# Two rows of a query weight kept on chip, and a new order of PV and scores, in a decode kernel that streams a KV cache

## The chip, the core and the metric

One core of a Trainium2 chip. The metric is the device time of one launch in microseconds. The kernel before takes 1152.5 us (median of 3 runs, 1148.8 to 1153.3).

A *ratio* below is the mean time of one kernel's fast runs over that of the kernel before in the same rounds, so it is not quite the ratio of the medians that are quoted with it. Differences in us are (ratio - 1) x 1152.

## The reference

```python
x = A_x                                        # 8 x 1 x 512
for _ in range(2):                             # two layers, same weights and same caches
    x = x + attn(layernorm(x), A_k_cache, A_v_cache, A_wq, A_wo)
    x = x + ffn(layernorm(x), B_w1, B_w2)      # silu(x @ w1) @ w2, 512 -> 1792 -> 512
# attn: 32 query heads, 8 KV heads, 8192 positions, head size 128, all 8 batches at one token
```

K and V are 134 MB each. The kernel reads K once for both layers, V twice, and runs the first layer of batch b+1 together with the second layer of batch b.

## The kernel before

All engines are filled from a static list. A planner in Python gives each piece of work a modelled duration and a priority, plays the kernel through, and the instructions are emitted in the order that comes out. Loads go out in a fixed order on one queue. V, `wo` and `wq` rows land in a ring of 7 cells of 512 KB (4 KB per partition); two neighbouring free cells may take one load of 1 MB. A cell comes free when the PV matmuls on it are done.

```python
N_CELL = 7
...
def load_wq(half, kt):          # one row of wq: 512 KB, one ring cell
    return load_cells(f"wq{half}.{kt}", 1, [(lambda buf: buf, wq_v[:, kt, GR * half:GR * (half + 1)])])
...
PARK = [(OT[0], ("ot", 0)), (OT[1], ("ot", 1)), (YT, ("yt",)), (EX, ("ex",))]   # spare halves of 4 PSUM banks
...
def queries_1(tag, prio, b0, nb, deps):         # queries of heads 16..31
    for kt in range(KT):                        # 4 rows of wq
        parked = kt == KT - 1 and nb == 1       # nb == 1: second layer of one batch
        wn = plan.reserve(f"{tag}.wq1") if parked else load_wq(1, kt)
        ...                                     # a parked row: 4 DVE transposes from PSUM to the cell
...
# in keys(): scores of one unit (batch, head group), four groups of 8 matmuls
sn.append(plan.add(f"s{u}.{q}", "PE", 0.45, score, pr - 1, [tn[3], bn] + sn[-1:]))
...
# in values(): PV of one unit, four groups of 8 matmuls, one for each cell
pr = count[0] - 1 if b < NB - 1 else u + 1
...
# in the planner: a node's followers become ready HOP = 0.1 us after it, on its own engine too
if what == "free":
    free[n.eng] = True
    heapq.heappush(events, (now + self.HOP, seq, "done", n))
```

## Time and profile before

| | before |
|---|---|
| time, median | 1152.5 us |
| profiled run: span, bytes on the queue | 1152.9 us (time 1154.7), 460.90 MB |
| busy: PE, DVE, ACT | 63%, 53%, 12% |
| queue's share of the 16 DMA engines | 98.1% |
| wq row loads into the ring | 28 |

The kernel streams: read the DMA and GB/s rows first, then ask in which stretches the rate is below the best. The prediction shows the lines.

### The profile page before, as it was taken

To read this page: it belongs to the slowest core of one execution; us is meant where nothing else is said; L and a number is where in the kernel's file an instruction comes from. 1 tells how busy PE (TensorE), PEld (TensorE's weight loads), DVE (VectorE), ACT (ScalarE), POOL (GpSimd) and SP (SyncE) were. 2 spreads that over 40 slices of the span, in tenths; PEclk is the share of its full clock that TensorE was granted. 3 is DMA by queue.
4 is the path that set the end of the run, shared out by engine and by line. 5 is a ranking of instruction groups with operands and counts; after the bars stand their busy time and mean duration, and the time that the engine had idled before them with its cause. 6 is when DMAs were issued, how large, how long until landed. Compare 5 with 4: busy or idle time off the path is not lost.

```text
span 1152.9 us, 32289 instructions
## 1 busy us (share of the span) xinstructions
PE 727.5 (63%) x13900; PEld 389.1 (34%) x13900; DVE 613.5 (53%) x1772; ACT 139.7 (12%) x485; POOL 116.8 (10%) x295
## 2 busy tenths in 40 slices
PE   2544565675665856656665766567566575665886
PEld 1322332342332433324332333234233243332544
DVE  5653467625674366634667255752566436663341
ACT  0010011101111110111111111110111111011111
POOL 1000111101110010100111000110011001010110
PEclk9655667757776676756767576765777566675675
DMA  9999899999999999999999999999999999999993
GB/s 368 419 422 399 326 416 424 413 403 409 423 417 411 396 423 418 417 389 412 417 419 417 397 417 419 419 410 394 417 421 417 403 412 421 415 419 396 369 424 135
DMA packets 78446, 462.96 MB, mean 402 GB/s; under 512 B 8400, under 2 KB 10208, under 8 KB 51936
## 3 DMA queue, kind: packets, MB, share of 16 engines
q1 hardware_dynamic: 78304, 460.90, 98.1%
q8 instruction: 109, 1.79, 0.6%
q14 instruction: 33, 0.27, 0.1%
HBM read 460.86 MB, written 0.01 MB: 400 GB/s over the span
## 4 chain that ended last, share of the span: by engine, by line
DMA 71%; PE 22%; issue 3%; DVE 2%; SPq 1%; POOL 1%; ACT 0%; POOLq 0%; DVEq 0%; ACTq 0%
DMA ring<-in_A_v_cache_dram 68%; PE ot L964 10%; PE sc L838 5%; DMA w<-in_B_w_dram 1%; PE misc L698 1%; PE misc L566 1%; DMA ring<-in_A_wq_dram 1%; PE misc L548 1%; PE yt L1038 1%; PE ex L986 1%; DVE part L978 0%; SPq L386 0%; PE sc L813 0%; POOL rstd L513 0%; PE ex L1008 0%
## 5 line engine op out<-in xcount | busy, mean ns | idle before, releaser
L964 PE MATMUL ot<-ring,p 128*8 128x256 bf16 x3904 | 246.1, 364 | 195.3 <-DMA ring<-in_A_v_cache_dram 191.3
L783 DVE STREAM_TRANSPOSE kts<-kts 128x1024 uint32<-128x1024 uint32 x256 | 308.5, 1225 | 32.1 <-DMA kts<-in_A_k_cache_dram 31.5
L838 PE MATMUL sc<-kts,bd 128*32 128x256 bf16 x4096 | 297.7, 406 | 38.9 <-DVE kts L783 32.8
L964 PEld LDWEIGHTS ot<-ring,p 128*8 128x8 bf16 x3904 | 79.1, 93 | 275.8 <-DMA ring<-in_A_v_cache_dram 247.4
L838 PEld LDWEIGHTS sc<-kts,bd 128*32 128x32 bf16 x4096 | 113.1, 118 | 109.3 <-DVE kts L783 45.7
L978 DVE TENSOR_TENSOR part<-ot,p 128x256 bf16<-128x256 f32 x128 | 54.2, 423 | 170.3 <-PE sc L838 80.4
L855 POOL PARTITION_ALL_REDUCE small<-small x128 | 47.6, 372 | 612.9 <-DVE small L851 382.0
L864 ACT ACTIVATE expd<-sc,small 128x256 bf16<-128x256 f32 x128 | 60.6, 473 | 403.9 <-DVE small L859 298.0
L974 ACT ACTIVATE p<-ot 128x256 bf16<-128x256 f32 x128 | 49.0, 383 | 458.1 <-PE ot L964 457.1
L870 PE MATMUL sc<-expd,ident 128*32 128x256 bf16 x512 | 43.1, 325 | 82.0 <-ACT expd L864 81.8
L884 POOL PARTITION_ALL_REDUCE small<-small x128 | 55.7, 435 | 213.8 <-DVE small L880 213.8
L877 DVE STREAM_TRANSPOSE p<-sc 128x256 bf16<-128x256 bf16 x128 | 56.6, 442 | 17.3 <-PE sc L870 13.8
L850 DVE TENSOR_REDUCE small<-sc 128x1 f32<-128x256 f32 x128 | 53.2, 416 | 18.1 <-PE sc L838 18.1
L821 DVE TENSOR_TENSOR bd<-sc,mask 128x64 bf16<-128x64 f32 x128 | 27.7, 216 | 54.9 <-PE sc L838 50.0
L870 PEld LDWEIGHTS sc<-expd,ident 128*32 128x32 bf16 x512 | 15.3, 110 | 110.7 <-ACT expd L864 109.2
L1015 DVE TENSOR_TENSOR z<-ex,rc 128x16 bf16<-128x16 f32 x72 | 12.5, 174 | 64.9 <-PE ex L1008 64.8
L880 DVE TENSOR_SCALAR small<-hm,small 128x4 f32<-128x4 f32 x128 | 26.6, 208 | 28.8 <-ACT expd L864 28.3
L986 PE MATMUL ex<-diag,p 128*128 128x4 bf16 x256 | 25.7, 169 | 25.4 <-DVE part L978 21.5
L986 PEld LDWEIGHTS ex<-diag,p 128*128 128x128 bf16 x256 | 16.9, 104 | 68.3 <-ACT p L974 41.5
L1038 PEld LDWEIGHTS yt<-z,ring 128*128 128x128 bf16 x1024 | 31.7, 102 | 24.2 <-issue 24.1
L1038 PE MATMUL yt<-z,ring 128*128 128x4 bf16 x1024 | 36.6, 166 | 4.7 <-DVE z L1015 4.3
L859 DVE SCALAR_TENSOR_TENSOR small<-small,hm 128x4 f32<-128x4 f32 x128 | 18.5, 144 | 26.4 <-POOL small L855 25.5
(96 smaller groups left out, 530.2 us busy)
## 6 DMA issues: line engine op xcount, KB each, us to landing
ring<-in_A_v_cache_dram SPq DMA_DIRECT2D x136, 1024.0 KB, 11.4
kts<-in_A_k_cache_dram SPq DMA_DIRECT2D x64, 2048.0 KB, 10.9
ring<-in_A_v_cache_dram SPq DMA_DIRECT2D x216, 512.0 KB, 7.5
ring<-in_A_wo_dram SPq DMA_DIRECT2D x64, 512.0 KB, 11.7
ring<-in_A_wq_dram SPq DMA_DIRECT2D x28, 512.0 KB, 10.4
kts<-in_A_v_cache_dram SPq DMA_DIRECT2D x5, 2048.0 KB, 23.9
kts<-in_A_wo_dram SPq DMA_DIRECT2D x2, 2048.0 KB, 16.4
w<-in_B_w_dram SPq DMA_DIRECT2D x2, 1792.0 KB, 13.7
```

The costliest lines, as they stand in the source:

```text
L783: op(dve, lambda: dve.transpose(v, v), reads=[], writes=[res("kt", g)], add=(q > 0))
L838: steps.append(lambda t=t, y=y, w=w: pe.matmul(sc[32 * t:32 * t + 32, 0:256], w, kv[:, 2 * t + y, q], start=(q == 0 and y == 0), stop=(q = ...
L850: op(dve, lambda: dve.tensor_reduce(mxr[si], sv, AX.X, ALU.max), reads=[res(*scr)], writes=[res("mxr", si)])
L864: op(act, lambda: act.activation(pe_out[:, :], sv, ACT.Exp, bias=bias[si], scale=SM_SCALE, accum_out=rsum[si]), reads=[res(*scr), res("bia ...
L870: steps = [lambda P=P: pe.matmul(sc[32 * P:32 * P + 32, 256:512], src[:, P], pe_out[:, :], start=True, stop=True) for P in range(4)]
L877: op(dve, lambda: dve.transpose(pt[:, :], src), reads=[res(*scr)], writes=[res("p", sm)])
L884: op(pool, lambda: pool.partition_all_reduce(ssa[si], ssm[si], 128, bass.bass_isa.ReduceOp.add), reads=[res("mxp", si)], writes=[res("mxa" ...
L964: steps.append(lambda t=t, c=c, k=k: pe.matmul(ot[32 * t:32 * t + 2 * R, 0:2 * DH], pt[:, k:k + 2 * R], vt[:, c, t], start=(P == 0 and c = ...
L974: op(act, lambda: act.activation(pt[:, :], ot[:, 0:2 * DH], ACT.Copy), reads=[res("ot", o)], writes=[res("p", sm)])
L978: op(dve, lambda: dve.tensor_tensor(part[:, :], ot[:, 0:2 * DH], pt[:, :], ALU.subtract), reads=[res("ot", o), res("p", sm)], writes=[res( ...
L986: steps.append(lambda k=k, src=src, y=y: pe.matmul(EX[:, 0:R], src[:, y * DH:y * DH + DH], diag[:, R * y:R * y + R], start=(k == 0 and y = ...
L1038: steps.append(lambda j=j, dt=dt: pe.matmul(YT[:, dt * R:(dt + 1) * R], w[:, j, dt * 128:(dt + 1) * 128], zt[:, R * j:R * j + R], start=(g ...
```

## The change

Its intent: fewer bytes, and cells that come back sooner.

1. Of the four rows of the second half of `wq`, two are kept on chip instead of one: in six pieces in spare columns of PSUM, and in 768 bytes per partition of SBUF. The exponential's own buffer, 512 bytes, was given up for these: the exponential now writes straight to its final buffer `p`. Two rows are loaded per batch, not three, and the four rows are used in a new order (3, 2, 0, 1).
2. They come back by four ACT copies and two DVE copies. Their cells are taken when they are needed (`extra`), not in the load order.
3. PV gets a better priority by three units: PV of landed values goes ahead of scores.
4. A node's followers on its own engine are ready at once, so the four score groups of a unit run through; their modelled duration goes from 0.45 to 0.5 us.
5. The first queries of a batch come in three groups instead of two.

```diff
+    def extra(self, name, emit, deps):                  # a cell without a load
...
             if what == "free":
                 free[n.eng] = True
+                for o in n.outs:
+                    if o.eng == n.eng:
+                        o.left -= 1
+                        if o.left == 0:
+                            heapq.heappush(heaps[o.eng], (o.prio, pending[id(o)], o))
...
-        for g0, g1 in ((0, 1), (1, 4)):
+        for g0, g1 in ((0, 1), (1, 2), (2, 4)):
...
+    PARK = [(3, 0, 256, OT[0], ("ot", 0), 256), (3, 256, 256, OT[1], ("ot", 1), 256),
+            (3, 512, 480, YT, ("yt",), 32), (3, 992, 32, EX, ("ex",), 480),
+            (2, 0, 448, EX, ("ex",), 32), (2, 448, 384, MI, ("misc",), 128)]
...
-        for kt in range(KT):
-            parked = kt == KT - 1 and nb == 1
+        rows = (3, 2, 0, 1)
+        for kt in rows:
+            kept_at = [i for i in range(len(PARK)) if PARK[i][0] == kt]
+            if kept_at and nb == 1:
+                wn = take_cell(kt, deps + list(behind))
...
-            sn.append(plan.add(f"s{u}.{q}", "PE", 0.45, score, pr - 1,
+            sn.append(plan.add(f"s{u}.{q}", "PE", 0.5, score, pr - 1,
...
-            op(act, lambda: act.activation(pe_out[:, :], sv, ACT.Exp, ...
+            op(act, lambda: act.activation(pt[:, :], sv, ACT.Exp, ...
...
-        pr = count[0] - 1 if b < NB - 1 else u + 1
+        pr = count[0] - 4 if b < NB - 1 else u + 1
```

More of the change, by code (lines that the diff above doesn't have):

```diff
@@ L118 @@
     __slots__ = ("eng", "dur", "emit", "prio", "deps", "outs", "left", "ready", "end", "take", "give", "name", "cells",
-                 "mate", "span")
+                 "mate", "span", "clear")
     def __init__(self, name, eng, dur, emit, prio, deps):
@@ L153, in __init__ @@
         self.loads = []
+        self.extras = []
     def add(self, name, eng, dur, emit, prio, deps=()):
@@ L167, in load @@
         return n
-    def reserve(self, name):
-        n = self.load(name, 1, lambda: None)
-        n.dur = 0
+    def extra(self, name, emit, deps):
+        n = Node(name, "DMA", 0, emit, 0, deps)
+        n.take = True
+        n.cells = 1
+        self.nodes.append(n)
+        self.extras.append(n)
         return n
@@ L198, in run @@
         loads = list(self.loads)
+        extras = list(self.extras)
         li = 0
@@ L211, in run @@
                 moved = False
+                for n in extras:
+                    at = self.place(idle, 1) if n.left == 0 else None
+                    if at is not None:
+                        extras.remove(n)
+                        n.give = at
+                        idle.discard(at)
+                        order.append((now, seq, n))
+                        seq += 1
+                        heapq.heappush(events, (now + self.HOP, seq, "done", n))
+                        seq += 1
+                        moved = True
+                        break
                 if li < len(loads):
@@ L242, in run @@
                         seq += 1
-                        if dur:
-                            wire = max(wire, now + 0.1) + dur
-                        heapq.heappush(events, (wire + self.LAND if dur else now + self.HOP, seq, "done", n))
+                        wire = max(wire, now + 0.1) + dur
+                        heapq.heappush(events, (wire + self.LAND, seq, "done", n))
                         seq += 1
@@ L277, in run @@
                 for o in n.outs:
+                    if o.eng == n.eng and n.eng != "DMA":
+                        continue
                     o.left -= 1
@@ L305, in _build @@
     NCH = 64
+    W1 = 384
     pe, dve, act, pool, sp = nc.tensor, nc.vector, nc.scalar, nc.gpsimd, nc.sync
@@ L337, in _build @@
     bds = [sb([128, 4 * 48], BF16, f"bd{i}") for i in range(N_BD)]
-    pe_out = sb([128, NCH * R], BF16, "expd")
+    wq1 = sb([128, W1], BF16, "wq1")
     ps = [sb([128, NCH * R], BF16, f"p{i}") for i in range(N_P + N_DEF)]
@@ L466, in norm_nodes @@
     def norm_nodes(tag, prio, b0, nb, deps):
-        nm = MI[:, 472:472 + nb]
-        st = MI[:, 480:480 + nb]
-        sq = MI[:, 488:488 + nb]
+        at = 40 if nb == 1 else 472
+        nm, st, sq = (MI[:, at + 8 * k:at + 8 * k + nb] for k in range(3))
         bs = slice(b0, b0 + nb)
@@ L539, in ffn_nodes @@
         hp = MI[:, 0:FT * nb]
-        yp = MI[:, 256:256 + KT * nb]
+        yp = MI[:, 32:32 + KT] if nb == 1 else MI[:, 256:256 + KT * nb]
         th, hs = (th1[:, :], hs1[:, :]) if nb == 1 else (big_th[:, 0:FT * nb], big_hs[:, 0:FT * nb])
@@ L709, in queries_0 @@
         return out_n
-    PARK = [(OT[0], ("ot", 0)), (OT[1], ("ot", 1)), (YT, ("yt",)), (EX, ("ex",))]
+    PARK = [(3, 0, 256, OT[0], ("ot", 0), 256), (3, 256, 256, OT[1], ("ot", 1), 256),
+            (3, 512, 480, YT, ("yt",), 32), (3, 992, 32, EX, ("ex",), 480),
+            (2, 0, 448, EX, ("ex",), 32), (2, 448, 384, MI, ("misc",), 128)]
     parks = []
-    def parked(i):
-        return PARK[i][0][:, 256:512].bitcast(U32)
-    def piece(wn, i):
-        n = GR // len(PARK)
-        return gran(wn.give)[:, n * i:n * (i + 1)].bitcast(U32)
@@ L722, in park @@
-    def park(i, wn):
-        op(dve, lambda: dve.transpose(parked(i), piece(wn, i)), reads=cells_of(wn), writes=[res(*PARK[i][1])])
-    def unpark(i, wn):
-        op(dve, lambda: dve.transpose(piece(wn, i), parked(i)), reads=[res(*PARK[i][1])],
-           writes=cells_of(wn), add=i > 0)
-    def queries_1(tag, prio, b0, nb, deps):
+    def park(i, wn):
+        row, w0, n, bank_, key, c0 = PARK[i]
+        op(dve, lambda: dve.tensor_scalar(
+            bank_[:, c0:c0 + n].bitcast(U32), gran(wn.give).bitcast(U32)[:, w0:w0 + n], 0, None, op0=ALU.bitwise_or),
+            reads=cells_of(wn), writes=[res(*key)])
+        if key == ("misc",):
+            op(dve, lambda: dve.tensor_copy(wq1[:, :], gran(wn.give)[:, GR - W1:GR]), reads=cells_of(wn), writes=[res("wq1")])
@@ new lines, in unpark @@
+    def unpark(i, wn, eng):
+        row, w0, n, bank_, key, c0 = PARK[i]
+        syn.acquire(eng, [wn.clear], [res(*key)])
+        if eng is act:
+            inst = act.activation(
+                gran(wn.give)[:, 2 * w0:2 * (w0 + n)], bank_[:, c0:c0 + n].bitcast(BF16), ACT.Copy)
+        else:
+            inst = dve.tensor_scalar(
+                gran(wn.give).bitcast(U32)[:, w0:w0 + n], bank_[:, c0:c0 + n].bitcast(U32), 0, None, op0=ALU.bitwise_or)
+        tok = syn.mark(inst, eng)
+        syn.release(tok, (), [res(*key)])
+        syn.release(tok, (), cells_of(wn), add=True)
@@ L732, in queries_1, with take_cell, emit @@
+    def take_cell(row, deps):
+        n = plan.extra(f"wq1.{row}", None, deps)
+        def emit():
+            n.clear = Res("clear")
+            for c in cells_of(n):
+                n.clear.writes += c.writes + c.reads
+                c.writes, c.reads = [], []
+        n.emit = emit
+        return n
+    def queries_1(tag, prio, b0, nb, deps, behind=()):
         qp = MI[:, 0:16 * nb]
         last = []
-        for kt in range(KT):
-            parked = kt == KT - 1 and nb == 1
-            wn = plan.reserve(f"{tag}.wq1") if parked else load_wq(1, kt)
-            filled = [wn]
-            if parked:
-                for i in range(len(PARK)):
-                    filled.append(plan.add(
-                        f"{tag}.unpark{i}", "DVE", 0.4, lambda i=i, wn=wn: unpark(i, wn), prio,
-                        [parks[i], filled[-1]]))
+        rows = (3, 2, 0, 1)
[3 more added lines that the diff above has]
+                wn = take_cell(kt, deps + list(behind))
+                eng, name = (act, "ACT") if kt == 3 else (dve, "DVE")
+                filled = [wn]
+                for i in kept_at:
+                    filled.append(plan.add(
+                        f"{tag}.unpark{i}", name, (0.3 + PARK[i][2] / 600) if eng is act else (0.1 + PARK[i][2] / 950),
+                        lambda i=i, wn=wn, eng=eng: unpark(i, wn, eng), prio, [wn, parks[i]] + filled[1:]))
+            else:
+                wn = load_wq(1, kt)
+                filled = [wn]
@@ L746, in mul @@
                 for h in range(16):
-                    steps.append(lambda h=h: pe.matmul(
-                        qp[:, h * nb:(h + 1) * nb], gran(wn.give)[:, h * DH:(h + 1) * DH], xn[:, b0:b0 + nb, kt],
-                        start=(kt == 0 and h == 0), stop=(kt == KT - 1), skip_group_check=True))
-                mms(steps, reads=cells_of(wn) + [res("xn")], writes=[res("misc")], add=kt > 0)
-            last = [plan.add(f"{tag}.r{kt}", "PE", 0.5, mul, prio, filled + deps + last)]
-            if kt == KT - 1 and nb > 1:
-                for i in range(len(PARK)):
-                    parks.append(plan.add(
-                        f"{tag}.park{i}", "DVE", 0.4, lambda i=i, wn=wn: park(i, wn), prio + 8,
-                        [wn, clear_n, last[0]] + parks[-1:]))
-                frees(parks[-1], wn)
+                    w = gran(wn.give)[:, h * DH:(h + 1) * DH]
+                    if kt == 2 and nb == 1 and (h + 1) * DH > GR - W1:
+                        w = wq1[:, h * DH - (GR - W1):(h + 1) * DH - (GR - W1)]
+                    steps.append(lambda h=h, w=w: pe.matmul(
+                        qp[:, h * nb:(h + 1) * nb], w, xn[:, b0:b0 + nb, kt],
+                        start=(kt == rows[0] and h == 0), stop=(kt == rows[-1]), skip_group_check=True))
+                mms(steps, reads=cells_of(wn) + [res("xn"), res("wq1")], writes=[res("misc")], add=kt != rows[0])
+            last = [plan.add(f"{tag}.r{kt}", "PE", 0.5, mul, prio, filled + deps + last)]
+            if kept_at and nb > 1:
+                done = last[0]
+                for i in kept_at:
+                    done = plan.add(f"{tag}.park{i}", "DVE", 0.1 + PARK[i][2] / 950, lambda i=i, wn=wn: park(i, wn),
+                                    prio + 8, [wn, clear_n, done])
+                    parks_of[i] = done
+                frees(done, wn)
             else:
                 frees(last[0], wn)
+        if nb > 1:
+            parks[:] = [parks_of[i] for i in range(len(PARK))]
         n = plan.add(f"{tag}.qc4", "DVE", 0.17, lambda: query_copy(4, 8, qp, nb), prio, last)
         return {g: n for g in range(4, 8)}
+    parks_of = {}
     count = [0]
     plain = [0]
-    last_exp = []
     sc_users = []
@@ L863, in exp @@
         def exp():
-            op(act, lambda: act.activation(pe_out[:, :], sv, ACT.Exp, bias=bias[si], scale=SM_SCALE, accum_out=rsum[si]),
-               reads=[res(*scr), res("bias", si)], writes=[res("expd"), res("rsum", si)])
+            op(act, lambda: act.activation(pt[:, :], sv, ACT.Exp, bias=bias[si], scale=SM_SCALE, accum_out=rsum[si]),
+               reads=[res(*scr), res("bias", si)], writes=[res("p", sm), res("rsum", si)])
         def swap():
@@ L870, in swap @@
             steps = [lambda P=P: pe.matmul(
-                sc[32 * P:32 * P + 32, 256:512], src[:, P], pe_out[:, :], start=True, stop=True) for P in range(4)]
-            mms(steps, reads=[res("ident"), res("expd")], writes=[res(*scr)])
+                sc[32 * P:32 * P + 32, 256:512], src[:, P], pt[:, :], start=True, stop=True) for P in range(4)]
+            mms(steps, reads=[res("ident"), res("p", sm)], writes=[res(*scr)])
         def back_in():
@@ L895, in keys @@
         n3 = plan.add(f"own{u}", "DVE", 0.17, own_max, pr - 1, [n2])
-        n4 = plan.add(f"exp{u}", "ACT", 0.42, exp, pr, [n3] + last_exp)
+        n4 = plan.add(f"exp{u}", "ACT", 0.42, exp, pr, [n3] + p_users.get(sm, []))
         n5 = plan.add(f"ss{u}", "DVE", 0.17, ssum, pr - 2, [n4])
         m4 = plan.add(f"sw{u}", "PE", 0.3, swap, pr - 2, [n4])
-        last_exp[:] = [m4]
-        n4 = plan.add(f"bk{u}", "DVE", 0.45, back_in, pr - 2, [m4] + p_users.get(sm, []))
+        n4 = plan.add(f"bk{u}", "DVE", 0.45, back_in, pr - 2, [m4])
         n6 = plan.add(f"sa{u}", "POOL", 0.45, sall, pr, [n5])
@@ L1064, in own @@
                 mask[:, :].unsqueeze(1).to_broadcast([128, R * nb, R]), ALU.mult),
-                reads=[res("ex"), res("mask")], writes=[res("ring", 1)])
+                reads=[res("mask")], writes=[res("ex"), res("ring", 1)])
         def mul():
@@ L1180, in advance @@
                     if g == 4:
-                        second_q.update(queries_1(f"c{b}", count[0] - 3, b, 1, [ready, second_q[3]]))
+                        second_q.update(queries_1(f"c{b}", count[0] - 3, b, 1, [ready, second_q[3]], scored[1]))
                     made[k] = keys(1, kb, g, second_q[g], held_units.index(k) if k in held_units else None, g == 0)
@@ L1203, in _build @@
     w = free_yt[0]
-    done = [h["n"] for h in ends] + [made[1]["n"]]
+    done = [h["n"] for h in ends] + [made[1]["n"], second_q[G - 1]]
     for g in range(G):
```

## The prediction

> **What bounds the kernel now.** I read the front page first: the slices, the DMA queue and the transfers.
>
> ```profile
> DMA  9999899999999999999999999999999999999993
> GB/s 368 419 422 399 326 416 424 413 403 409 423 417 411 396 423 418 417 389 412 417 419 417 397 417 419 419 410 394 417 421 417 403 412 421 415 419 396 369 424 135
> ...
> q1 hardware_dynamic: 78304, 460.90, 98.1%
> ...
> ring<-in_A_v_cache_dram SPq DMA_DIRECT2D x136, 1024.0 KB, 11.4
> ...
> ring<-in_A_v_cache_dram SPq DMA_DIRECT2D x216, 512.0 KB, 7.5
> ring<-in_A_wo_dram SPq DMA_DIRECT2D x64, 512.0 KB, 11.7
> ring<-in_A_wq_dram SPq DMA_DIRECT2D x28, 512.0 KB, 10.4
> ```
>
> The 16 DMA engines are full in all slices but the fifth and the last, and they move 460.90 MB. No compute engine is near that: PE is busy 63% of the span, DVE 53%, ACT 12%. Bytes divided by rate therefore give most of the 1152.9 us. The next view, stretches of 20 us, shows where they do not; its last three columns are the granted PE clock, the DMA share and GB/s.
>
> ```profile
> 100.00:120.00 20.00, 9.46 (x237) 6.85 (x238) 3.19 (x13) 1.32 (x6) 1.15 (x2) 0.50 0.99 373
> 120.00:140.00 20.00, 11.79 (x236) 6.78 (x236) 9.26 (x25) 1.78 (x6) 1.62 (x4) 0.67 0.77 311
> ...
> 420.00:440.00 20.00, 12.46 (x229) 6.89 (x232) 12.77 (x35) 2.45 (x8) 2.03 (x5) 0.69 1.02 419
> ...
> 500.00:520.00 20.00, 12.81 (x245) 6.10 (x241) 4.66 (x19) 2.44 (x9) 1.40 (x3) 0.50 1.01 379
> ...
> 640.00:660.00 20.00, 13.72 (x299) 7.41 (x300) 3.82 (x16) 2.09 (x8) 1.03 (x2) 0.56 1.01 401
> ...
> 1080.00:1100.00 20.00, 17.92 (x344) 9.45 (x348) 9.09 (x46) 3.91 (x14) 3.21 (x8) 0.83 0.98 355
> ...
> 1120.00:1140.00 20.00, 15.78 (x359) 10.04 (x359) 3.62 (x15) 2.48 (x9) 1.53 (x1) 0.50 0.68 283
> 1140.00:1160.00 20.00, 6.17 (x164) 4.92 (x162) 2.53 (x9) 0.94 (x4) 0.55 (x1) 0.63 0.00 1
> ```
>
> Three levels are to be seen. Where K and paired V come in (2 MB and 1 MB), the rate is about 419. Where single cells of 512 KB come in, around the change from one batch to the next, it is about 400 although the share is still 1.01. Real holes are few: about 5 us in 120 to 140 (one minus 0.77, times 20; rate 311), about 2 us in 100 to 120, about 3 us in 1080 to 1100 (one minus 355/419, times 20), and the end. In 1120 to 1140 the rate of 283 gives 5.66 MB, at 420 some 13.5 us, so the last bytes land near 1134. The kernel ends at 1152.9: a tail of about 19 us in which DMA does nothing.
>
> **What holds the queue.** The waits of the DMA queue itself:
>
> ```profile
> SPq L91 <- PE ot L964: 582.0, 285, 19.9
> SPq L386 <- PE sc L838: 121.6, 19, 14.2
> SPq L91 <- PE yt L1038: 43.3, 22, 2.8
> ```
>
> The issuing sequencer spends half the span waiting for PV matmuls to give ring cells back. This looks like the bound, but it is back-pressure: with a share of 1.0 the engines still have earlier transfers to do while the sequencer waits. Only where the share or the rate drops is such a wait worth time.
>
> **What the Trainium skill says.** "DMA: Bandwidth & Descriptors", section "Rules for kernel authors", asks for 128 partitions and at least 1 MiB per DMA for the best bandwidth. The trace agrees in direction: 419 against 401 GB/s, a loss of 4% for 512 KB; so a saved wq row is dearer than its bytes suggest. "Perfetto Trace Analysis", section "Optimization Strategy", says to look for the gaps on the most contended engine; that is what the second view was for. "ScalarE: Activation LUTs", section "What ACT_TABLE_LOAD costs", gives an ACTIVATE with immediate scale and bias as 186 ns + 0.833 N. At N = 256 that is 399 ns; the copy of PV's result (128x256) takes 383 ns here, so I use it for the new ACT copies. "PSUM — Partial Sum Buffer", section "PSUM bank collisions raise a hardware error", says to guard PSUM by bank and quadrant, not by address: copies out of spare columns must be ordered against the matmuls that write other columns of that bank. The code does acquire the bank; no run so far shows what that wait costs.
>
> **The change part by part.**
>
> (a) *Bytes.* Before, one of the four rows of the second half of wq was parked in PSUM and three were loaded for each batch: 4 at the start plus 8 times 3 = 28, as the transfer list has it. After, two are kept. The issue order of the changed kernel has 20. Eight transfers of 524,288 bytes go: 4.19 MB, at 400 GB/s 1.31 us each, 10.5 us together. The order also has V in 133 pairs and 222 singles where it was 136 and 216: six singles more (7.9 us) for three pairs less (3 x 2.50 = 7.5 us), +0.4 us. Net -10.1 us on an engine that is full there, so this comes off the end nearly whole. w1 and w2 are loaded by the same two statements in both kernels; I give that nothing.
>
> (b) *Unparking.* Before: four DVE transposes of 128x256 words for each batch, 32 x about 408 ns = 13 us in all. After: four ACT copies (512, 512, 960 and 64 elements: by the formula 0.61, 0.61, 0.99, 0.24, an estimate of 2.45 us per batch, 20 us in all) and two DVE copies of 448 and 384 words (estimate from the transposes of 256 words at 408 ns: 0.6 us each, 10 us in all). ACT goes from 139.7 to about 160 us busy, DVE falls slightly. The cells for them are taken when they are needed, after the first scores of the batch, instead of in the load order; in the new order this puts the next V pair a few instructions later, right behind a 2 MB K load that covers 5 us. I give 0 to +1 us per batch at worst, 0 as the centre.
>
> (c) *Order on PE.* PV of landed cells now goes before scores, and the four score groups of a unit run together. This gives cells back sooner. It is worth only what starvation there is: in the batch changes (379 in 500 to 520 against 400 possible is 1 us; others less) and in 1080 to 1100 (3 us). I count -2 us. The hole at 120 to 140 stays: there are no held units to fill the first feed-forward, and the new order has the same two V pairs and then the same K load that waits for the first unit's scores.
>
> (d) *The tail.* The timeline of the end before:
>
> ```profile
> 1130.70 1.65 PE L566 MATMUL misc<-ring,w 128*128 128x7 bf16 x56
> ...
> 1132.29 1.45 PE L964 MATMUL ot<-kts,p 128*8 128x256 bf16 x24
> ...
> 1136.49 1.45 PE L964 MATMUL ot<-kts,p 128*8 128x256 bf16 x24
> ...
> 1139.98 0.60 PE L964 MATMUL ot<-kts,p 128*8 128x256 bf16 x8
> ...
> 1143.37 0.17 DVE L1109 TENSOR_REDUCE ysum<-yt 128x4 f32<-128x16 f32 x1 [0.68 <-PE yt L1038]
> ```
>
> The last value quarter is in by about 1134, but its 8 matmuls run at 1139.98: PE is about 6 us behind with PV of the last three units and with the other seven batches' feed-forward put between. In the new order, all 32 PV matmuls of the third last unit stand before that feed-forward's first half, and 64 instead of 96 PV matmuls follow it. If PE keeps up, the last PV follows its landing within 1.5 us and the tail shrinks by about 4.5 us; the chain behind it (3.4 us to the sum, 9.5 us of feed-forward and output) stays. PE is busy 17.9 of 20 us just before, so it may not keep up: I count -2.5.
>
> Sum: 1152.5 - 10.1 + 0 - 2 - 2.5 = about 1138.
>
> **The rivals.** *Only the bytes count* (the tail order is eaten by PE at its low clock, 0.50 in that window; ring cells were never the limit): 1142. For it: share 1.01 almost everywhere. Against it: the 6 us lag at the end is real, and the order view shows a real change there. *Cells become the bound*: two cells held for unparking while ACT does 2.4 us of copies behind its exponentials, PE's scores of later units blocked behind an in-order wq matmul, each batch starving DMA by 2 us: 8 x 2 = 16 us lost, 1154. For it: the 582 us of waits for cells show how tight the ring is. Against it: before, loaded rows held their cells some 10 us each from issue to landing, so two loaded plus two short-lived cells ask for less than three plus one. *The order pays more than I think*: all batch changes rise to 400 to 405, the 3 us near 1085 vanish, the first hole shrinks by half and the tail by 4.5: about 1152.5 - 10.1 - 6 - 3 - 4.5 = 1129, just at 2%.
>
> **Range and chances.** The bytes are nearly certain and make 0.9%. The range runs from most of the third rival to somewhat worse than the first: 1131 to 1147, which also covers the 4.6 us spread of the three runs before. Over 2% faster means below 1129.5, possible only if every side effect pays: 0.08. Over 2% slower would need 23 us of new waiting on top of the lost saving: 0.02.
>
> **What would show it.** Right: 456.7 MB on the queue, 20 wq transfers in the ring, the same level of about 419 and 400 in the same kinds of stretch, last bytes near 1122 to 1124, and the last PV within 2 us of them. (c) wrong: 1080 to 1100 still near 355. (d) wrong: still 18 us or more after the last bytes. The whole is wrong if the DMA share falls below 0.95 in stretches with unparking, or if the queue's waits show a new line for ACT or for the clearing of a wq cell.

## More of the kernel before

One more view is needed for the result, and the prediction did not have it: the stretches in which one batch gives way to the next. I bounded them by K loads, whose 16,384-byte packets can be told apart: from the landing of a batch's last K to that of the next batch's first. Here are four of the six, in the kernel before; the columns are the stretch, its length, busy us and instructions of PE, PE's weight loads, DVE, ACT and POOL, then the granted PE clock, the DMA share and GB/s.

```profile
217.10:269.30 52.20, 34.19 (x684) 18.38 (x684) 17.67 (x62) 6.41 (x22) 4.38 (x10) 0.62 1.01 400
...
491.10:542.80 51.70, 34.63 (x684) 18.25 (x684) 17.58 (x62) 6.33 (x22) 4.37 (x10) 0.57 1.01 397
628.40:678.60 50.20, 34.13 (x684) 18.41 (x684) 17.60 (x62) 6.33 (x22) 4.38 (x10) 0.60 1.02 404
...
901.10:951.80 50.70, 33.69 (x684) 18.65 (x684) 17.56 (x61) 6.33 (x22) 4.38 (x10) 0.60 1.02 408
```

To be seen: the DMA share says "full" in all of them, while the rate differs by 11 GB/s between stretches that move the same kinds of transfer. The share alone does not tell the faster stretch from the slower.

## The result, and the profile after

1148.8 us (median of 4 runs, 1148.0 to 1149.8) against 1151.6 in the same rounds: ratio 0.9978, 95% interval 0.9955 to 1.0001. A second measurement in other rounds gave 0.9964 (0.9945 to 0.9983). So the change is worth 2.5 to 4 us (the first interval just includes none), not the 14 that I predicted, and the time lies above my range.

From the page of the changed kernel, the queue and its transfers:

```profile
q1 hardware_dynamic: 77584, 456.70, 98.0%
...
ring<-in_A_v_cache_dram SPq DMA_DIRECT2D x133, 1024.0 KB, 11.7
...
ring<-in_A_v_cache_dram SPq DMA_DIRECT2D x222, 512.0 KB, 7.3
...
ring<-in_A_wq_dram SPq DMA_DIRECT2D x20, 512.0 KB, 12.2
```

The bytes went as predicted: 4.20 MB less, 20 wq loads, 133 pairs and 222 singles. Stretches of 20 us of the changed kernel, to be set against those in the prediction:

```profile
120.00:140.00 20.00, 12.90 (x273) 7.74 (x270) 10.46 (x29) 3.73 (x10) 1.62 (x4) 0.59 0.76 294
...
640.00:660.00 20.00, 14.93 (x344) 8.77 (x347) 4.03 (x17) 1.92 (x7) 1.15 (x2) 0.50 1.02 401
...
1060.00:1080.00 20.00, 17.22 (x428) 11.93 (x429) 6.34 (x27) 4.05 (x11) 1.38 (x3) 0.59 0.91 343
```

The hole of the first change of batch is as deep as before, and the dip of 1080 to 1100 has moved to 1060 to 1080 and is no smaller: 343 against 355. (A second profile of the changed kernel, e10 below, has 375 there and 367 in the next 20 us.) The batch changes of the changed kernel, the same four:

```profile
216.20:268.10 51.90, 34.67 (x716) 19.24 (x716) 18.39 (x64) 8.28 (x26) 4.38 (x10) 0.63 1.02 400
...
488.40:539.20 50.80, 34.12 (x696) 18.83 (x696) 18.23 (x63) 8.34 (x26) 4.02 (x10) 0.59 1.01 390
623.60:675.00 51.40, 33.69 (x716) 19.16 (x716) 18.95 (x65) 8.39 (x26) 4.38 (x10) 0.65 1.02 403
...
894.90:946.50 51.60, 34.61 (x716) 19.31 (x716) 18.34 (x64) 8.28 (x26) 4.34 (x10) 0.60 1.01 394
```

Two of the four are 7 and 14 GB/s slower than before, at a nearly unchanged share. The six stretches together are as long as before (307.6 us, before 307.8) but move 0.8 MB less. The third and the sixth are slow in both profiles of this kernel (e10 has 393 and 380 GB/s over the packets of these two), so this goes with its list and is not chance alone.

**Where the time went.** The table cuts each profile at K landings. "Steady" is from a batch's third K to its last, seven stretches; "change" from there to the third K of the next, six stretches; "end" from the last K to the last V byte, "tail" from there to the end of the span. MB are what landed in the stretch. All are worked out from the packets of one profile per kernel.

| us (MB) | to last K of batch 0 | first change | 6 changes | 7 steady | end | tail | span |
|---|---|---|---|---|---|---|---|
| before | 86.0 | 72.0 | 465.0 (189.2) | 414.4 (172.4) | 97.8 | 17.8 | 1152.9 |
| changed | 86.2 | 73.0 | 467.9 (189.2) | 404.7 (168.3) | 99.0 | 16.3 | 1147.1 |
| changed, again | 86.3 | 73.4 | 468.1 (189.1) | 405.9 (168.7) | 97.1 | 15.6 | 1146.4 |

Seven of the eight saved wq loads fall into the steady stretches, the eighth into the end. In the steady stretches the bytes pay in full: -9.7 us for 4.1 MB (-8.5 for 3.7 MB in the second profile), as the prediction's term (a) has it. Then 2.9 us are given back in the six changes, 1.0 in the first change and 1.2 in the end, although the end has one load less, and the tail gains 1.5. The sum is 0.2 + 1.0 + 2.9 - 9.7 + 1.2 - 1.5 = -5.9, which is the difference of the two profiled spans. The profile of before is one of its slower runs, so the medians differ by less, and some of the 2.9 and 1.2 may be the scatter of single profiles.

The copies that bring rows back cost what was estimated; busy us, mean ns of one:

```profile
L752 ACT ACTIVATE ring<-ot 128x512 bf16<-128x512 bf16 x16 | 8.8, 595 | 18.8 <-PE ot L1019 18.7
L752 ACT ACTIVATE ring<-yt 128x960 bf16<-128x960 bf16 x8 | 7.8, 972 | 0.0
L755 DVE TENSOR_SCALAR ring<-ex 128x448 uint32<-128x448 uint32 x8 | 5.0, 620 | 0.5 <-PE ot L1019 0.4
```

595 and 972 ns against 610 and 990 estimated, 620 against 600 for the DVE copy; ACT is at 155.1 us busy, predicted 160.

**One pause seen closely.** The last use of the parked rows, from the timeline of the changed kernel (start, length, engine, line, operation):

```profile
1066.97 1.93 SPq L410 DMA_DIRECT2D ring<-in_A_wq_dram  x2
...
1067.88 0.60 PE L1019 MATMUL ot<-ring,p 128*8 128x256 bf16 x8
...
1070.57 1.56 PE L894 MATMUL sc<-kts,bd 128*32 128x256 bf16 x24
...
1071.93 1.12 PE L1019 MATMUL ot<-ring,p 128*8 128x256 bf16 x21
...
1075.34 8.87 SPq L410 DMA_DIRECT2D ring<-in_A_v_cache_dram  x8
```

L1019 is PV, L894 the scores. Between the PV group at 1067.88 and the next at 1071.93 PE does two query groups and the scores of the first unit, 24 matmuls of them in one piece. No cell comes back in that time, and two cells are held by the wq loads. The first two cells that come back go to the parked rows: their copies start at 1072.97 (DVE) and 1073.08 (ACT). The sequencer issues nothing from 1068.90 to 1075.34, and these 6.4 us lie in the stretch with 343 GB/s; 1.9 us of them are a gap in the middle of PE's PV group, in which PE waits for nothing that the profile shows (the last section comes back to it).

e16 below has the same kept rows, PE's old ordering rules, and is the fastest correct kernel:

```profile
1061.08 2.07 SPq L403 DMA_DIRECT2D ring<-in_A_wq_dram  x2
...
1069.19 7.31 SPq L403 DMA_DIRECT2D ring<-in_A_v_cache_dram  x8
```

```profile
1065.38 0.63 PE L1012 MATMUL ot<-ring,p 128*8 128x256 bf16 x8
...
1066.24 0.63 PE L1012 MATMUL ot<-ring,p 128*8 128x256 bf16 x8
```

There L1012 is PV and parts the scores, so two cells come back early, but the next V load still waits until 1069.19: the copies of the parked rows start at 1066.53 and 1067.49. The pause after the last wq load is 6.0 us in e16, 6.0 in e3 and 6.1 in e18 (old rules), 6.4 and 5.4 in the two profiles of the changed kernel, and 4.0 to 5.8 in all other variants with two kept rows. With one kept row it is 1.7 us in the kernel before (1077.10 to 1078.80; its longest pause near there is 2.9) and 1.0 in e4, which has the new rules (3.8 at its longest). So this pause goes with the two kept rows and their late cells, and not with the order on PE.

### The profile page after: what moved, and what is told of

It is laid out like the page before. It is cut to its first block, busy times and chain, and to the rows that moved or that the text cites. A ratio compares the mean times of both kernels' runs of the same rounds, so it can differ in the third digit from the quotient of the medians.

```text
span 1147.1 us, 32316 instructions
## 1 busy us (share of the span) xinstructions
PE 719.4 (63%) x13900; PEld 390.2 (34%) x13900; DVE 609.9 (53%) x1768; ACT 155.1 (14%) x517; POOL 116.9 (10%) x295
## 3 DMA queue, kind: packets, MB, share of 16 engines
q8 instruction: 109, 1.79, 0.6%
## 5 line engine op out<-in xcount | busy, mean ns | idle before, releaser
L1019 PE MATMUL ot<-ring,p 128*8 128x256 bf16 x3904 | 236.9, 365 | 168.8 <-DMA ring<-in_A_v_cache_dram 155.9
L894 PE MATMUL sc<-kts,bd 128*32 128x256 bf16 x4096 | 284.3, 406 | 45.8 <-DVE kts L839 38.3
L1019 PEld LDWEIGHTS ot<-ring,p 128*8 128x8 bf16 x3904 | 82.1, 95 | 243.5 <-DMA ring<-in_A_v_cache_dram 205.9
L894 PEld LDWEIGHTS sc<-kts,bd 128*32 128x32 bf16 x4096 | 114.3, 117 | 121.9 <-DVE kts L839 53.0
L920 ACT ACTIVATE p<-sc,small 128x256 bf16<-128x256 f32 x128 | 60.7, 474 | 368.5 <-DVE small L915 153.6
L926 PE MATMUL sc<-p,ident 128*32 128x256 bf16 x512 | 42.9, 324 | 105.6 <-ACT p L920 105.1
L933 DVE STREAM_TRANSPOSE p<-sc 128x256 bf16<-128x256 bf16 x128 | 56.7, 443 | 10.5 <-PE sc L926 8.9
L926 PEld LDWEIGHTS sc<-p,ident 128*32 128x32 bf16 x512 | 15.5, 111 | 134.7 <-ACT p L920 133.1
L869 PE MATMUL sc<-qab,ident 128*128 128x4 bf16 x256 | 18.3, 177 | 27.9 <-DVE p L933 24.4
L1041 PEld LDWEIGHTS ex<-diag,p 128*128 128x128 bf16 x256 | 16.5, 105 | 56.1 <-issue 31.0
## 6 DMA issues: line engine op xcount, KB each, us to landing
kts<-in_A_k_cache_dram SPq DMA_DIRECT2D x64, 2048.0 KB, 10.9
```

The lines of the kernel that those rows point to most:

```text
L894: steps.append(lambda t=t, y=y, w=w: pe.matmul(sc[32 * t:32 * t + 32, 0:256], w, kv[:, 2 * t + y, q], start=(q == 0 and y == 0), stop=(q = ...
L920: op(act, lambda: act.activation(pt[:, :], sv, ACT.Exp, bias=bias[si], scale=SM_SCALE, accum_out=rsum[si]), reads=[res(*scr), res("bias", ...
L926: steps = [lambda P=P: pe.matmul(sc[32 * P:32 * P + 32, 256:512], src[:, P], pt[:, :], start=True, stop=True) for P in range(4)]
L933: op(dve, lambda: dve.transpose(pt[:, :], src), reads=[res(*scr)], writes=[res("p", sm)])
L1019: steps.append(lambda t=t, c=c, k=k: pe.matmul(ot[32 * t:32 * t + 2 * R, 0:2 * DH], pt[:, k:k + 2 * R], vt[:, c, t], start=(P == 0 and c = ...
```

## The experiments

All ran with five rounds (6 fast runs each) beside the kernel before. Three theories were on record for the first set: **O**, the new order on PE starves the ring at the changes; **C**, the cells taken for parked rows do; **B**, bytes do not pay in full because the queue is held by cells.

**e3_order_back**: the two kept rows (with what came with them: the exponential's new target, the new row order, the late cells), all ordering parts as before. The diff is shortened.

```diff
-                for o in n.outs:                 # followers on the same engine at once
-                    if o.eng == n.eng: ...
-        for g0, g1 in ((0, 1), (1, 2), (2, 4)):
+        for g0, g1 in ((0, 1), (1, 4)):
-  plan.add(f"s{u}.{q}", "PE", 0.5,     pr = count[0] - 4
+  plan.add(f"s{u}.{q}", "PE", 0.45,    pr = count[0] - 1
```

> The changed kernel with every ordering part undone: the same-engine rule, the PV priority, the modelled score duration and the split of the first queries are as before; only the two kept rows and the exponential written straight to p stay. Theory O: the whole byte saving shows, -8 to -11 us against before. Theory C: -2 to -4, as the changed kernel. Theory B: -2 to -4.

Measured: 1143.8 us, ratio 0.9927 (0.9902 to 0.9953), -8.4 us. The parked rows and their cells are all still there, so C and B do not hold as they were put: neither must eat the saving. e18 below weakens this: with another list these same parts saved 1.4 us.

**e4_order_alone**: the ordering parts put on the kernel before, bytes unchanged. The unpark copies acquire their PSUM bank as in the changed kernel, so e4 has these waits too, and is not the order alone.

> The kernel before with the ordering parts alone (same-engine rule, PV priority, score duration, split of the first queries) and one parked row as before; the unpark copies wait for their bank, or the check finds a bank conflict. Same bytes as before. Theory O: slower by 4 to 8 us. Theory C and theory B: within 2 us of before.

Measured: 1156.7 us, ratio 1.0032 (1.0005 to 1.0059), +3.7 us. Together with e3: -8.4 + 3.7 = -4.7, near the -2.5 to -4.1 of the whole; each is one list, so the agreement may be luck. (Its profile fell on its fastest run, 1152.0, and does not show the loss.)

**e1_no_through**: the changed kernel without the same-engine rule.

> The changed kernel with one rule of its scheduler taken back: a node's followers on the same engine become ready 0.1 us after it again, so that the four score groups of a unit can be parted by PV. All else of the change stays (two kept rows, 133 V pairs or about that, PV priority). Theory O (the new order on PE starves the ring at batch changes and gives the saved bytes back): -7 to -10 us against before. Theory C (cells taken for unparking give them back): no better than the changed kernel, -2 to -4. Theory B (fewer bytes do not pay in full, because the queue is held by ring cells and not by bytes): -2 to -4.

Measured: 1147.7 us, ratio 0.9961 (0.9933 to 0.9988), -4.5 us. No better than the changed kernel. So the scores that run through are not shown to cost anything; e8 below has them too and saves 9.6 us.

**e5_bytes_alone**: the kernel before, 24 wq loads cut to 1360 of 2048 columns, so as many bytes less as the change saves.

```diff
-            wn = ... else load_wq(1, kt)
+            wn = ... else load_wq(1, kt, 1360 if nb == 1 else GR)
```

> The kernel before, in its own order, with the 24 wq loads of the batches cut from 2048 to 1360 columns: 24 x 688 x 2 x 128 bytes = 4.23 MB less, as much as the change saves, with no other cell or wait changed. Results are wrong on purpose (the rest of those cells is stale). Theory O and theory C: the bytes pay, -9 to -11 us. Theory B: -2 to -5 us.

Measured: 1145.4 us, ratio 0.9940 (0.9915 to 0.9964), -6.9 us: between what was expected of B and of the others. The interval, -4.1 to -9.8, leaves out the 10.6 us that 4.23 MB cost at 400 GB/s, so in this order the bytes did not pay quite in full. (The comparison with the reference passed although parts of the weights were stale, so that comparison is blind to the second half of the second layer's queries.)

**e10_after_again, e2_pv_prio, e8_split_back, e9_through_prio_back**: the changed kernel unaltered; with `pr = count[0] - 1`; with the split of the first queries and the score duration as before; with rule and priority as before.

> The changed kernel unaltered, to have it in the same rounds as the parts. If its first measurement (-0.2%) was typical: -2 to -4 us. If it was a slow draw and the order costs nothing: -7 to -9 us, as with the order taken back.

> The changed kernel with the PV priority alone taken back. If PV ahead of the scores of three units is what costs: -6 to -8 us. If it is neutral: as the changed kernel, -2 to -4.

> The changed kernel with the first queries in two groups again and the modelled score duration 0.45. If the split of the first queries costs (scores of the first unit come sooner and hold PV back at the batch change): -5 to -8 us. If neutral: -2 to -4.

> The changed kernel with the same-engine rule and the PV priority taken back together. If these two are the whole cost of the order: -7 to -9 us, as with all four parts taken back (-8). If each part carries a share: -5 to -6.

| | median us | ratio (95%) | us |
|---|---|---|---|
| e10, unaltered | 1148.5 | 0.9964 (0.9945 to 0.9983) | -4.1 |
| e2, priority back | 1156.9 | 1.0031 (1.0002 to 1.0061) | +3.6 |
| e8, split and duration back | 1143.2 | 0.9917 (0.9896 to 0.9938) | -9.6 |
| e9, rule and priority back | 1146.3 | 0.9952 (0.9930 to 0.9974) | -5.5 |

Both of my expectations for e2 were wrong: in this list, where scores run through, taking PV's priority away costs 8 us. Two batch changes of e2:

```profile
353.50:407.50 54.00, 34.47 (x716) 19.73 (x716) 18.47 (x65) 8.50 (x26) 4.38 (x10) 0.59 0.98 372
...
629.60:682.60 53.00, 33.56 (x716) 18.79 (x716) 18.37 (x64) 8.50 (x26) 4.01 (x9) 0.64 0.99 380
```

372 and 380 GB/s where the changed kernel has 404 and 403. e8 looked like the culprit found: 5 us in the split or the duration. The next set asked which, and whether that is a cause at all: e13 and e14 move a constant that has nothing to do with the change.

**e11_only_split_back, e12_only_duration_back, e13_after_jitter, e14_e8_jitter**

```diff
-T_TURN = 1.23        # e13, e14: modelled us of one K transpose, in the planner alone
+T_TURN = 1.26
```

> The changed kernel with only the split of the first queries taken back (score duration in the scheduler stays 0.5). The order of the transfers is then the same as in the changed kernel, and PE's nearly so. If the split costs the 5 us that came back in the run with split and duration taken back: -8 to -10 us against before. If the cost lies in the schedule that the duration of 0.5 makes: -3 to -5.

> The changed kernel with only the score duration in the scheduler back at 0.45 (the split stays). Split theory: -3 to -5 us. Duration theory: -8 to -10 us.

> The changed kernel with a constant of the scheduler that has nothing to do with the change moved a little (modelled duration of a K transpose 1.23 to 1.26 us). Split or duration theory: stays at -3 to -5 us. Lottery theory (any new list order moves the time by some us, and the changed kernel drew a poor one): may land anywhere from 0 to -10.

> The kernel with split and duration taken back (-9.5 us), with the same unrelated constant moved to 1.26. Split or duration theory: stays at -8 to -10 us. Lottery theory: moves by 3 us or more, likely for the worse.

| | median us | ratio (95%) | us |
|---|---|---|---|
| e11, split back | 1148.8 | 0.9969 (0.9942 to 0.9996) | -3.6 |
| e12, duration back | 1145.0 | 0.9938 (0.9913 to 0.9963) | -7.1 |
| e13, changed, constant moved | 1149.0 | 0.9972 (0.9946 to 0.9999) | -3.2 |
| e14, e8, constant moved | 1149.0 | 0.9966 (0.9937 to 0.9995) | -3.9 |

The split is neutral. The duration seemed to be it (e12), but e14 has the old duration too and is back at -3.9: an unrelated 0.03 us in the planner took away what "the cause" had given. The two traces show the same loads in the same order, and only PE's order differs. The difference is 5.7 us with an uncertainty of about 4 (from the two intervals; each was measured beside the kernel before, on different chips). So e8 was a good draw of the list, and the theory that names one part falls.

**e15_before_jitter, e16_e3_jitter, e17_after_half_rows, e6_six_cells_before**: the constant moved in the kernel before and in e3; the changed kernel, in exactly its own order, with the 16 wq loads that are left cut to half; the kernel before with `N_CELL = 6`.

> The kernel before with the unrelated constant moved (K transpose 1.23 to 1.26 us in the scheduler). Lottery theory: anywhere within 6 us of before, not the same. Theory that before's order is tuned and any other is worse: slower by 3 to 8 us.

> The kernel with all ordering parts taken back (-8.4 us) with the same constant moved. If the old ordering rules are simply better: stays at -7 to -10. Lottery theory: moves by 3 us or more, to between -3 and -6.

> The changed kernel in its own, unaltered order, with the 16 wq loads that are left in the batches cut to half their columns: another 4.19 MB less. Wrong results on purpose. If bytes pay in the steady stretches in any order: -7 to -10 us further, so -10 to -14 against before. If this order is held by ring cells rather than bytes: at most -3 further, -4 to -7 against before.

> The kernel before with six ring cells instead of seven. If cells are what starves DMA at the batch changes: slower by 10 us or more, with the loss mainly between the last K of one batch and the first ones of the next, and rates under 400 GB/s there. If cells are not scarce: within 3 us.

| | median us | ratio (95%) | us |
|---|---|---|---|
| e15, before, constant moved | 1151.0 | 0.9991 (0.9966 to 1.0015) | -1.0 |
| e16, e3, constant moved | 1142.9 | 0.9910 (0.9891 to 0.9928) | -10.4 |
| e17, changed, 4.19 MB less | 1138.9 | 0.9878 (0.9855 to 0.9900) | -14.1 |
| e6, before, six cells | 1194.2 | 1.0352 (1.0322 to 1.0382) | +40.6 |

e17 speaks against theory B. In the changed kernel's own order another 4.19 MB are worth 14.1 - 4.1 = 10.0 us, near the full price at 400 GB/s (10.5), with an uncertainty of about 3.4. Between the profiles, 6.3 us are saved in the steady stretches, 3.6 in the end and 1.6 in the six changes, and 1.6 are lost at the start. So bytes pay in this order. e6 shows how scarce the cells are. One cell less costs 40 us; between the profiles, 24.6 of 44 us lie in the six changes, 9.7 in the steady stretches and 7.8 in the end. Its changes run at:

```profile
224.40:281.00 56.60, 34.23 (x684) 18.60 (x684) 17.70 (x62) 6.43 (x22) 4.38 (x10) 0.56 0.96 362
369.70:424.30 54.60, 34.15 (x684) 18.40 (x684) 17.46 (x62) 6.43 (x22) 4.38 (x10) 0.62 0.99 369
```

while the fastest correct kernel, e16, has in the same places:

```profile
217.10:268.70 51.60, 34.84 (x716) 18.94 (x716) 18.26 (x63) 8.39 (x26) 4.38 (x10) 0.63 1.01 403
353.10:403.10 50.00, 34.57 (x716) 19.11 (x716) 18.40 (x64) 8.27 (x26) 4.37 (x10) 0.63 1.02 403
```

**e18_e3_jitter_down, e19_after_jitter_down**: the constant moved the other way, to 1.20, in e3 and in the changed kernel, to see whether the old rules are better in general.

> The kernel with all ordering parts taken back, scheduler constant 1.20 instead of 1.23. Theory that the old rules keep the saving: -7 to -11 us against before. Lottery theory: -3 to -6 as likely as more.

> The changed kernel, the same constant 1.20. Theory that the new rules lose it: -2 to -5 us. Lottery theory: -6 to -10 as likely as less.

Measured: e18 1149.8 us, ratio 0.9988 (0.9965 to 1.0010), -1.4 us; e19 1148.9 us, ratio 0.9969 (0.9945 to 0.9993), -3.6 us. The old rules do not keep the saving in general either: -8.4, -10.4, -1.4 under three values of the constant (the step from -8.4 to -10.4 is within the noise, that to -1.4 is not). The new rules give about -3.3 (the mean of its two measurements), -3.2 and -3.6.

**What the profiles of all runs say together.** The same cut as above:

| us | 6 changes | 7 steady | us in the six last-K-to-first-K stretches with under 1.1 MB queued |
|---|---|---|---|
| before | 465.0 | 414.4 | 14.9 |
| changed; again | 467.9; 468.1 | 404.7; 405.9 | 14.4; 16.9 |
| e2, priority back | 475.9 | 405.3 | 31.9 |
| e14 | 473.0 | 405.8 | 16.5 |
| e8 | 465.1 | 404.5 | 10.1 |
| e16 | 462.7 | 405.0 | 8.3 |
| e6, six cells | 489.6 | 424.1 | 57.4 |

The last column is the time in which the bytes issued so far less the bytes moved so far were under 1.1 MB (a "thin" queue), sampled every 0.1 us. Every variant with two kept rows and whole wq loads has its steady stretches within 3 us of 405; most of the differences between them lie in the changes (462 to 476 us for nearly the same bytes). Over the 19 profiles with seven cells, the time with a thin queue correlates with the length of those last-K-to-first-K stretches at 0.81 (0.68 without e2). The end varies too (95.4 to 99.2 us), and single profiles scatter by some us (that of e14 is its slowest run, 1153.4 against a median of 1149.0), so this shows the place; it does not price each order.

The thin queue is not the cause of the changed kernel's loss, though. Its time is the same before and after (14.9 and 14.4 us), and the rate within it is hardly lower: 388 GB/s in the changed kernel, against 397 in the rest of those stretches (390 and 400 before). That is worth some 0.4 us. In the stretch at 390 GB/s, 488.4 to 539.2, only 5 us are thin, and the rate outside them is 389. Even in e2 (356 in the thin moments, 388 in the rest) and e6 (348 and 378) it makes by the same sum 2.6 of the 10.9 us and 4.5 of the 24.6 us that their changes take longer than before. What lowers the rate while enough is queued, no run here shows.

## Why the prediction was wrong

- **(a), the bytes: right.** Predicted -10.1; the steady stretches show -9.7 and -8.5 in two profiles of the changed kernel, and e17 shows another 10.0 for the next 4.19 MB (e5, in the order of before, 6.9). The remark that a saved wq row is dearer than its bytes did not come true: 9.7 us for 4.1 MB is the steady stretches' own rate, about 420 GB/s.
- **(b), unparking: right in its durations, too low at the last use.** e3 and e16 have the copies and the late cells and still save 8 and 10 us, so it does not cost 2 us in each batch, as the rival had it. But the last use holds the queue for 5.4 to 6.4 us where the kernel before has 1.7; I had allowed 1 us at worst. How much of it reaches the end is not shown.
- **(c), the order on PE: the step that failed.** I wrote "This gives cells back sooner. It is worth only what starvation there is" and counted -2. In its place: 2.9 us more in the six changes, 1.0 more in the first and 1.2 more at the end, +5 in all in the profile (the pause of (b) is part of the last); the ordering parts cost +3.7 on the kernel before (e4, interval 0.6 to 6.8). The new order brought nothing in any place that I named: the dip is at 343, the changes are no faster. Why is open. That scores that run through hold PE where the ring is tightest, as I thought, is not shown: without that rule nothing is gained (e1, -4.5), and e8 has it and saves 9.6. What the runs show is that lists with the same loads and different PE orders lie 6 us apart (e8 and e14), so the order that a list happens to have outweighs the -2 that I gave to the rules.
- With it stood a reading of the profile that was too strong: "with a share of 1.0 the engines still have earlier transfers to do". The share is 1.01 at 390 GB/s and at 408, so it does not tell where the rate drops. I named "cells become the bound" as a rival and gave it 1154, 2 us in each batch for cells held for unparking. That cells are scarce is shown (e6, +40.6 us); that loss in each batch is not.
- **(d), the tail: right in kind, mis-sized.** -2.5 predicted, -1.5 and -2.2 in the two profiles. The new order puts fewer PV matmuls behind the other batches' feed-forward, as read from the listing, but PE is still late:

```profile
1130.40 1.42 PE L589 MATMUL misc<-ring,w 128*128 128x7 bf16 x48 [0.58 <-issue]
...
1133.66 1.02 PE L1019 MATMUL ot<-kts,p 128*8 128x256 bf16 x16
...
1137.48 0.17 DVE L1164 TENSOR_REDUCE ysum<-yt 128x4 f32<-128x16 f32 x1 [0.68 <-PE yt L1093]
```

The last V byte lands at 1130.75, and its eight matmuls, the second half of the group at 1133.66, begin at 1134.04: the rest of the feed-forward's second half and three earlier PV groups of eight stand in between. That is 3.3 us of lag; I had hoped for 1.5. Before, the last V byte landed at 1135.15 and not near 1134, so the lag was 4.8 us and not 6, and there was less to gain.

- **The range** was too narrow on the upper side for a reason that I could have seen: a static list made by a greedy planner is a different list after any edit. A step of 0.03 us in an unrelated constant moved e8 by 5.7 us and e3 by +7.0 in one direction and -2.0, within the noise, in the other. A prediction of such a kernel needs a term of several us for the redrawn list alone.

**What stays open.** Whether the new ordering rules are worse than the old ones on average. Three values of the constant give means of -6.7 and -3.4 with two kept rows, but the old rules' three values span 9 us. Which feature of a list makes a change of batch slow is open too: the thin queue accounts for a small part. Each variant is one list, or two or three, so no part of the change has a price of its own here.

**A version that beats both:** e16, two kept rows with the old ordering rules and the constant at 1.26, at 1142.9 us (-0.9% against before); e8 is as good (1143.2). Both are draws, not designs.

## What to carry to other kernels

A saving on the saturated resource is real (here 4.2 MB were 7 to 10 us where nothing else was changed, e5 and e17), but look for it by stretches, because what a change does elsewhere can eat it: the total alone said "nothing happened". A DMA share near 1 does not mean the best rate: compare the rate between stretches that move the same kind of transfer. When you suspect a thin queue, count bytes issued less bytes moved, and then compare the rate inside and outside the thin moments before you call it the cause. Look for a pause that you blame on a change in the fast variants too. And where a scheduler makes the list, move an unrelated constant before you believe that a part of the change is the cause.

## What the Trainium skill lacked or had wrong

- "Perfetto Trace Analysis", section "Identifying the Most-Contended Engine", says that occupancy of the DMA engines misleads and that HBM utilization should be used. It is right, and I did not heed it enough: the share was 1.01 at 390 GB/s and at 421 in the same kernel. What no page has is why the rate falls at a full share: in the stretch at 390 it was 389 while more than 1.1 MB was queued. The runs do not tell either.
- "DMA: Bandwidth & Descriptors", section "Bandwidth", gives 341 GB/s for a transfer of 1 MB, measured per transfer. It has no figure for transfers of this size queued one behind the other: here the stretches of mainly 512 KB transfers reach about 400 and those of 1 and 2 MB about 419. The section "Specifications" lists about 358 GB/s as the limit of HBM per core; it is not wrong, since "Bandwidth" says that this is the share when both cores of the pair stream. One core alone held 413 to 421 here in stretches of 57 us and more.
- "ScalarE: Activation LUTs", section "What ACT_TABLE_LOAD costs": nothing is wrong; its formula for an ACTIVATE held for copies from PSUM (613 ns by the formula against 595 for 512 elements, 986 against 972 for 960).
- The gaps of over 1 us in which PE waits for nothing that the profile shows (1.92 and 1.42 us near the end of the changed kernel, 1.64 in the kernel before): there are 25 in the 20 profiles, and every one ends 1.2 to 1.6 us after a 16 KB packet of queue q8, which the profile calls "instruction", has landed. Such packets come about every 10.5 us. The 109 of them in the kernel before are 1.79 MB, or 64 bytes for each of PE's 27,800 matmuls and weight loads. So PE most likely waits there for its own instructions; no run tests it, and most packets pass without such a gap. It belongs to "Runtime: NRT & Kernel Launch", section "Instruction fetch mechanics", which gives no time for such a wait.
